# A cached attention decode step beside a squared-ReLU MLP: fewer key blocks scored on TensorE, products for 52 blocks on GpSimd

## The chip, the core and the metric

The kernel runs on one core of a Trainium2 chip. The metric is the time of one execution on the device, in microseconds; lower is better. The kernel before takes 193.13 us, the median of three runs (193.12 to 193.56).

## The reference

One token `x` of 512 values goes through two branches, which a scalar gate mixes.

```python
g = sigmoid((x * gate_w).sum(-1))
q = (x @ wq) as 32 heads of 128
scores = einsum("hd,hkd->hk", q, k_cache) * 128 ** -0.5     # 4096 keys a head
o = einsum("hk,hkd->hd", softmax(scores), v_cache)
a = o as 4096 values @ wo                                   # 4096 x 512
h = relu(x @ w1 + b1); b = (h * h) @ w2 + b2                # 512 -> 1376 -> 512
out = g * a + (1 - g) * b
```

All inputs are bf16. The K and V caches hold 32 MB each (4 MB for four heads), wq and wo 4 MB each, w1 and w2 1.4 MB each. Every byte is used once.

## The kernel before

**Quads.** The 32 heads are worked on four at a time: eight quads. The 128 partitions of a quad's K tile hold four heads of 32 partitions, and each partition holds 128 keys of 128 values, so a "block" is one key of each partition: 128 blocks a quad. V lies in the same way. K has three buffers (`Kt`), V two (`Vt`). The third K buffer first holds the MLP weights, the second V buffer wq, the first V buffer at the end wo, and the V tiles of the last two quads go into K buffers.

**Scores.** A score is the product of a key with the q of its head, summed over 128 values. It is made in two ways. For 48 blocks (`XB`) VectorE multiplies K by q, which is spread over the head's partitions in `qb` (`prods`, line 574, two times 24 blocks), and sums over the 128 values (`sums`, line 583). For the other 80 TensorE transposes a block (`transposes`, line 395), ScalarE moves eight transposed blocks at a time from PSUM to `kT` (`evac`, line 321), and TensorE multiplies each with the four q columns in `qc` (`scores`, line 405); VectorE copies that part of the scores out of PSUM (line 590) and takes the row maxima (line 597).

**Softmax and PV.** TensorE and VectorE bring the maxima of a head's 32 partitions together (`max_rows`, `gmax`, `max_cols`), ScalarE copies the negative maximum (line 325) and forms the exponentials and their sums (line 336), and TensorE multiplies V blocks by them (`pv`, line 437). At the end the denominators are summed (`den`, line 448), the result is normalised and regrouped (lines 636 to 641), and TensorE multiplies it with wo in five pieces (`attn_out`, line 506), each waiting for its own DMA. The last steps are `fin` (line 644), a transpose, a copy, and the DMA of 1 KB.

**q.** The q of all heads is first made as columns (128 matmuls, line 372), copied to `qc`, transposed, and spread over partitions by eight matmuls with the selector `selq`; ScalarE copies the result to `qb` (line 315).

**The MLP.** The 1376 hidden units are held as 8 columns of 128, one of 96 and 8 of 32 (`FG`, `FR`, `TX` by `QX`). The last, 256 rows of w2, are the extras: they are loaded as 32 rows of eight w2 rows (8 KB) into partitions 0 to 15 and 32 to 47 of `WX` by 8 DMAs with four rows each (line 252). `mlp_h` (lines 462 and 466) makes the units, VectorE's `mlp` squares them, `mlp_x` moves the extras to their partitions with the selector `selh`, and `mlp_out` (line 487) adds to the output. Its end (`s_ml`) releases the third K buffer.

**What sets the order.** Each engine follows a list written out by hand, with semaphores between engines. SP issues all large loads in this order: wq, K0, w1, w2 with its extras, K1, V0, K2 (waits for `s_ml`), K3, V1, K4, V2, K5, V3, K6, V4, K7, V5, V6, V7 in two halves, wo in five pieces. From K3 on, a K load waits until its buffer's quad has been transposed and multiplied (lines 221 and 222); a V load waits for the PV of two quads before (line 232). TensorE runs transposes and scores of quad i chunk by chunk, and between the chunks the max steps of quad i-1 and the PV of quads i-2 and i-3. VectorE works on quad i's products and sums with the maxima of quad i-1 in between. GpSimd only prepares constants in the first 9 us.

Of the kernel before, what the change touches and what calls it, by code (L numbers as in the profile page):

```python
# [5 lines left out]
def bass_gated_mix__gqa_block_cached__dense_activation_squared_relu__decode_kernel(  # L6
# [30 lines left out]
    FG = 8  # L37
    FR = 96
    F0 = FG * 128
    F1 = F0 + FR  # L40
    TX = 8
    QX = 32
    PX = 48
# [3 lines left out]
    XB = 48  # L47
    XH = XB // 2
# [8 lines left out]
    NR = 5  # L57
# [15 lines left out]
    with ctx:  # L73
# [18 lines left out]
        pr = sb("pr", [128, XH, 128], fp32)  # L92
        qb = sb("qb", [128, NQ, 128], bf16)
        qT = sb("qT", [NH, 128], bf16)
        selq = sb("selq", [NH, NQ, 128], bf16)
# [42 lines left out]
        pS = [pb(f"pS{i}", [128, 512], fp32) for i in range(2)]  # L138
# [8 lines left out]
        Q = pX[:, 0:NH]  # L147
# [4 lines left out]
        QR = [T[1], T[2]]  # L152
# [4 lines left out]
        def S(i):  # L157
            return pS[i % 2][:, 0:4 * YB].rearrange("p (b h) -> p b h", h=4)
# [24 lines left out]
        s_q = sem("s_q")  # L183
# [6 lines left out]
        s_qb = sem("s_qb")  # L190
        s_mu = sem("s_mu")
        s_sd = sem("s_sd")
# [22 lines left out]
        with nc.Block() as block:  # L215

            @block.sync
            def _(eng):
                def load_k(i):
                    if i >= NK:  # L220
                        eng.wait_ge(s_t, NC * (i - NK + 1))
                        eng.wait_ge(s_mu, 2 * (i - NK + 1))
# [4 lines left out]
                def load_v(i):  # L227
                    if i == 1:
                        eng.wait_ge(s_q, 1)
# [6 lines left out]
                    eng.wait_ge(s_mu, 2 * i)  # L236
# [32 lines left out]
            def _(eng):  # L269
# [4 lines left out]
                eng.memset(selq[:, :, :], 0.0).then_inc(s_id, 1)  # L274
                eng.memset(sel[:, :, :], 0.0).then_inc(s_id, 1)
                eng.memset(selm[:, :], -SCALE).then_inc(s_id, 1)
                eng.wait_ge(s_id, 6)
                for m in (ident, identf):
# [3 lines left out]
                eng.affine_select(out=selq[:, :, :], in_=selq[:, :, :], compare_op=ALU.not_equal, fill=1.0,  # L282
                                  base=0, pattern=[[-4, NQ], [-1, 4], [0, HP]], channel_multiplier=1)\
                   .then_inc(s_id, 1)
# [3 lines left out]
                eng.wait_ge(s_id, 10)  # L288
# [7 lines left out]
                for p, q in ((0, 0), (32, 16)):  # L296
                    eng.affine_select(out=selh[:, p:p + 16], in_=selh[:, p:p + 16], compare_op=ALU.not_equal,
                                      fill=1.0, base=-q, pattern=[[-1, 16]], channel_multiplier=1)\
                       .then_inc(s_hx, 1)

            @block.scalar
            def _(eng):
# [7 lines left out]
                eng.activation(xcol[:, :], xcolf[:, :], ACT.Copy).then_inc(s_xf, 1)  # L310
                eng.wait_ge(s_z, 1)
                eng.activation(ez[:, :], Z, ACT.Exp, scale=-1.0).then_inc(s_ez, 1)
                for g in range(2):
                    eng.wait_ge(s_qr, g + 1)
                    eng.activation(qb[:, 4 * g:4 * g + 4, :], QR[g][:, :].rearrange("p (j d) -> p j d", d=128), ACT.Copy).then_inc(s_qb, 1)  # L315

                def evac(n):
                    eng.wait_ge(s_t, n + 1)
                    if n >= NR:
                        eng.wait_ge(s_sc, n - NR + 1)  # L320
                    eng.activation(kT[:, n % NR, :], T[n % NT][:, :].bitcast(bf16), ACT.Copy).then_inc(s_ev, 1)  # L321

# [4 lines left out]
                def exps(j, hs_):  # L327
                    if hs_[0] == 0:
                        eng.wait_ge(s_nm, j + 1)
                        if j == 0:  # L330
                            eng.wait_ge(s_id, 13)
                        if j >= NE:
                            eng.wait_ge(s_pv, j - NE + 1)
                    for h in hs_:
# [5 lines left out]
                for i in range(NQ + 1):  # L340
                    for c in range(NC):
# [13 lines left out]
            def _(eng):  # L355
# [159 lines left out]
                for n in range((NQ + LAG) * NC):  # L515
                    i, c = n // NC, n % NC
                    if n < N:
                        transposes(n)
# [157 lines left out]
```

## Time and profile before

| | |
|---|---|
| median of the runs | 193.13 us |
| profiled execution | 193.35 us |
| its span | 192.1 us |
| HBM read | 78.32 MB, 408 GB/s over the span |
| TensorE, VectorE, ScalarE, GpSimd busy | 134.9, 134.7, 102.4, 7.9 us |
| mean granted TensorE clock | 0.663 |

A busy engine in this profile is one with an instruction in work; its waits are named by what released it. "DMA" in the slices and windows is the mean busy share of the core's 16 DMA engines. In the chain of work, the program is followed back from its last instruction, each time to what released it. DVE is VectorE, ACT ScalarE, PE TensorE and POOL GpSimd.

### The profile page before, as it was taken

How to read it: one execution, taken by the hardware profiler on the slowest of the kernel's cores; microseconds unless marked ns; L12 is line 12 of the kernel's file. 1: busy time of each engine (PE TensorE's matmuls, PEld its weight loads, DVE VectorE, ACT ScalarE, POOL GpSimd, SP SyncE). 2: the span in 40 equal slices, each digit the busy share in tenths (PEclk: the TensorE clock that was granted, in tenths of full speed). 3: DMA queues.
4: the chain of work that ended last, by engine and by line, in shares of the span. 5: the costliest groups of instructions: out<-in, count | busy, mean ns of one | idle time of the engine just before them, and what ended most of it. 6: DMA issues, size and time to landing. Idle time of an engine off the chain costs nothing.

```text
span 192.1 us, 6115 instructions
## 1 busy us (share of the span) xinstructions
PE 134.9 (70%) x2768; PEld 130.3 (68%) x2768; DVE 134.7 (70%) x157; ACT 102.4 (53%) x159; POOL 7.9 (4%) x21
## 2 busy tenths in 40 slices
PE   0128089997803996589979397939794988667954
PEld 0126089997703995579979397939794988667943
DVE  6410095999993999999999899939993899440010
ACT  2101050869961989637947766586648574904000
POOL 8800000000000000000000000000000000000000
PEclk9999999997885699555555555555555555555555
DMA  6999999999999999999999999999999999999981
GB/s 219 438 437 437 391 448 430 437 420 437 433 427 418 418 433 423 427 430 433 427 413 437 433 437 427 427 430 433 423 440 425 427 430 433 396 423 403 421 328 45
DMA packets 3823, 78.70 MB, mean 410 GB/s; under 512 B 467, under 2 KB 565, under 8 KB 822
## 3 DMA queue, kind: packets, MB, share of 16 engines
q1 hardware_dynamic: 3784, 78.32, 95.9%
q8 instruction: 21, 0.34, 0.7%
q14 instruction: 4, 0.03, 0.0%
q10 hardware_dynamic: 14, 0.01, 0.0%
HBM read 78.32 MB, written 0.00 MB: 408 GB/s over the span
## 4 chain that ended last, share of the span: by engine, by line
DMA 70%; PE 16%; DVE 11%; SPq 1%; issue 1%; DVEq 0%
DMA Kt<-in_A_k_cache_dram 40%; DMA Vt<-in_A_wo_dram 16%; DMA Kt<-in_B_w_dram 13%; PE T L395 7%; DVE pr L574 5%; DVE Sb L583 4%; PE pX L466 2%; PE pO L437 2%; PE pS L405 1%; DVE mp L597 1%; PE pX L487 1%; DVE Sb L590 1%; PE pX L462 1%; SPq L263 1%; PE pX L506 1%
## 5 line engine op out<-in xcount | busy, mean ns | idle before, releaser
L321 ACT ACTIVATE kT<-T 128x1024 bf16<-128x1024 bf16 x80 | 80.3, 1025 | 50.8 <-PE T L395 50.1
L395 PE MATMUL T<-ident,Kt 128*128 128x128 bf16 x640 | 74.3, 290 | 24.2 <-DMA Kt<-in_A_k_cache_dram 23.1
L395 PEld LDWEIGHTS T<-ident,Kt 128*128 128x128 bf16 x640 | 56.7, 131 | 25.1 <-DMA Kt<-in_A_k_cache_dram 23.6
L574 DVE TENSOR_TENSOR pr<-Kt,qb 128x3072 f32<-128x3072 bf16 x16 | 53.7, 3357 | 17.9 <-DMA Kt<-in_A_k_cache_dram 17.0
L583 DVE TENSOR_REDUCE Sb<-pr 128x12 f32<-128x1536 f32 x32 | 55.1, 1745 | 0.5
L405 PEld LDWEIGHTS pS<-qc,kT 128*128 128x128 bf16 x640 | 30.9, 111 | 4.4 <-ACT kT L321 4.4
L405 PE MATMUL pS<-qc,kT 128*128 128x4 bf16 x640 | 30.9, 170 | 3.5 <-ACT kT L321 3.2
L437 PE MATMUL pO<-E,Vt 128*128 128x4 bf16 x768 | 28.8, 166 | 3.8 <-DMA Vt<-in_A_v_cache_dram 3.8
L437 PEld LDWEIGHTS pO<-E,Vt 128*128 128x128 bf16 x768 | 25.5, 103 | 4.5 <-issue 4.0
L336 ACT ACTIVATE E<-Sb,nM 32x128 bf16<-32x128 f32 x32 | 18.4, 576 | 0.9
L590 DVE COPY Sb<-pS 32x80 f32<-32x80 f32 x32 | 7.5, 236 | 3.8 <-PE pS L405 3.0
L597 DVE TENSOR_REDUCE mp<-Sb 32x1 f32<-32x128 f32 x32 | 8.9, 277 | 1.6
L336 ACT ACTIVATION_READ_ACCUMULATOR E<-Sb,nM 32x1 f32 x32 | 8.0, 250 | 0.0
L437 PE MATMUL pO<-E,Kt 128*128 128x4 bf16 x256 | 7.3, 166 | 0.0
L437 PEld LDWEIGHTS pO<-E,Kt 128*128 128x128 bf16 x256 | 7.2, 105 | 0.0
L416 PE MATMUL pM<-identf,mp 128*4 128x128 f32 x8 | 2.9, 360 | 5.8 <-DVE mp L597 5.8
L315 ACT ACTIVATE qb<-T 128x512 bf16<-128x512 f32 x2 | 1.1, 594 | 9.1 <-PE T L381 9.1
L359 PE MATMUL pM<-ident,xrow 1*128 1x1 bf16 x4 | 0.3, 165 | 7.9 <-POOL sel L292 7.9
L359 PEld LDWEIGHTS pM<-ident,xrow 1*128 1x128 bf16 x4 | 0.2, 108 | 7.9 <-POOL sel L292 7.9
L506 PE MATMUL pX<-o,Vt 128*128 128x1 bf16 x128 | 3.9, 165 | 1.6 <-DMA Vt<-in_A_wo_dram 1.3
L506 PEld LDWEIGHTS pX<-o,Vt 128*128 128x128 bf16 x128 | 3.6, 104 | 1.9 <-DMA Vt<-in_A_wo_dram 1.5
L416 PEld LDWEIGHTS pM<-identf,mp 128*4 128x4 f32 x8 | 0.7, 82 | 6.1 <-DVE mp L597 6.1
(75 smaller groups left out, 61.6 us busy)
## 6 DMA issues: line engine op xcount, KB each, us to landing
Kt<-in_A_k_cache_dram SPq DMA_DIRECT2D x8, 4096.0 KB, 29.4
Vt<-in_A_v_cache_dram SPq DMA_DIRECT2D x6, 4096.0 KB, 21.7
Vt<-in_A_wq_dram SPq DMA_DIRECT2D x1, 4096.0 KB, 12.5
Kt<-in_A_v_cache_dram SPq DMA_DIRECT2D x1, 4096.0 KB, 32.2
Kt<-in_A_v_cache_dram SPq DMA_DIRECT2D x2, 2048.0 KB, 31.3
Vt<-in_A_wo_dram SPq DMA_DIRECT2D x3, 1024.0 KB, 27.6
Kt<-in_B_w_dram SPq DMA_DIRECT2D x1, 1376.0 KB, 25.8
Kt<-in_B_w_dram SPq DMA_DIRECT2D x1, 1024.0 KB
```

The source lines that it names most:

```text
L321: eng.activation(kT[:, n % NR, :], T[n % NT][:, :].bitcast(bf16), ACT.Copy).then_inc(s_ev, 1)
L336: eng.activation(E[a:b, j % NE, :, h], Sb[a:b, j % NS, :], ACT.Exp, bias=nM[a:b, j:j + 1], scale=SCALE, accum_out=RS[a:b, j:j + 1]).then_i ...
L395: mm = eng.transpose(T[n % NT][:, :].bitcast(bf16)[:, y * 128:(y + 1) * 128], Kt[:, i % NK, w * 128:(w + 1) * 128], ident[:, :])
L405: mm = eng.matmul(S(i)[:, c * TC + y, :], kT[:, n % NR, y * 128:(y + 1) * 128], qc[:, 4 * i:4 * i + 4], start=True, stop=True)
L416: eng.transpose(MT, mp[:, i, :], identf[:, :]).then_inc(s_mt, 1)
L437: mm = eng.matmul(pO[:, 4 * i:4 * i + 4], VT(i)[:, y * 128:(y + 1) * 128], E[:, i % NE, y, :], start=(y == 0), stop=(y == NB - 1))
L466: mm = eng.matmul(H[0:height(n), n:n + 1], units(w1_t[:, t, :], n), xcol[:, t:t + 1], start=False, stop=(t == 3), skip_group_check=True)
L506: mm = eng.matmul(acc[:, j:j + 1], wo_sb[:, t, j * 128:(j + 1) * 128], o2[:, t:t + 1], start=False, stop=(t == 31), skip_group_check=True)
L574: eng.tensor_tensor(pr[:, :, :], Kt[:, i % NK, u * XH * 128:(u + 1) * XH * 128] .rearrange("p (b d) -> p b d", b=XH), qb[:, i:i + 1, :].br ...
L583: eng.tensor_reduce(Sb[:, i % NS, u * XH + a:u * XH + b], pr[:, a:b, :], AX.X, ALU.add)\
L590: eng.tensor_copy(Sb[a:b, i % NS, XB:NB], S(i)[a:b, :, h]).then_inc(s_cp, 1)
L597: eng.tensor_reduce(mp[a:b, i, h:h + 1], Sb[a:b, i % NS, :], AX.X, ALU.max)\
```

## The change

Five things change together.

- The blocks of a quad are divided anew: GpSimd multiplies 52 blocks by q (four times 13, into two buffers `pg`), VectorE multiplies 28 (two times 14) and sums all 80, and TensorE transposes and scores 48 instead of 80 (six chunks instead of ten).
- VectorE's products read q from PSUM (`PQ`, a copy made once a quad), not from SBUF. The scores of TensorE's blocks have one PSUM bank instead of two and are copied out by ScalarE, not VectorE.
- q is made spread over the partitions from the start: ScalarE writes x into all 128 weight columns (`xb`), four matmuls of 512 columns a quad give q on every partition, ScalarE copies 32 partitions of each head to `qb`, and transposes of `qb` give the columns. The selector `selq` goes.
- The MLP's units become 9 columns of 128, one of 64 and 4 of 40; the w2 extras become 40 rows of four w2 rows (4 KB), loaded by 8 DMAs with five rows each.
- TensorE's order becomes plain: all transposes and scores of quad i, the max steps of quad i-1, PV of quad i-2. In quad 0 the MLP stands behind all transposes and scores. ScalarE and VectorE are ordered to suit.

```diff
-    FG = 8
-    FR = 96
+    FG = 9
+    FR = 64
-    TX = 8
-    QX = 32
-    PX = 48
+    TX = 4
+    QX = 40
+    PX = 52
-    XB = 48
-    XH = XB // 2
+    GP = 4
+    GB = 13
+    XP = 2
+    XH = 14
+    XB = GP * GB + XP * XH
...
-    NR = 5
+    NR = 4
...
+        pg = sb("pg", [128, 2, GB, 128], fp32)
+        xb = kT[:, 0, 0:512].rearrange("p (t n) -> p t n", t=4)
...
-        pS = [pb(f"pS{i}", [128, 512], fp32) for i in range(2)]
+        pS = pb("pS", [128, 512], fp32)
+        pQ = pb("pQ", [128, 512], fp32)
...
                     if i >= NK:
                         eng.wait_ge(s_t, NC * (i - NK + 1))
-                        eng.wait_ge(s_mu, 2 * (i - NK + 1))
+                        eng.wait_ge(s_mu, XP * (i - NK + 1))
+                        eng.wait_ge(s_pm, GP * (i - NK + 1))
...
-                    for p, q in ((0, 0), (32, 16)):
-                        eng.dma_start(WX[p + r:p + 16:4, :], w2_x[q + r:q + 16:4, :]).then_inc(s_w2, 16)
+                    for p, q in ((0, 0), (32, 20)):
+                        eng.dma_start(WX[p + r:p + 20:4, :], w2_x[q + r:q + 20:4, :]).then_inc(s_w2, 16)
...
+                for i in range(NQ):
+                    eng.wait_ge(s_k[i % NK], 16 * (i // NK + 1))
+                    eng.wait_ge(s_qb, 4 * (i + 1))
+                    for k in range(GP):
+                        n = GP * i + k
+                        if n >= 2:
+                            eng.wait_ge(s_ps, n - 1)
+                        eng.tensor_tensor(pg[:, n % 2, :, :], Kt[:, i % NK, k * GB * 128:(k + 1) * GB * 128]
+                                          .rearrange("p (b d) -> p b d", b=GB),
+                                          qb[:, i:i + 1, :].broadcast_to([128, GB, 128]), ALU.mult)\
+                           .then_inc(s_pm, 1)
...
+                eng.activation(xb, xcolf[:, :].rearrange("p (t o) -> p t o", o=1).broadcast_to([128, 4, 128]),
+                               ACT.Copy).then_inc(s_xf, 1)
...
-                for g in range(2):
-                    eng.wait_ge(s_qr, g + 1)
-                    eng.activation(qb[:, 4 * g:4 * g + 4, :], QR[g][:, :].rearrange("p (j d) -> p j d", d=128), ACT.Copy).then_inc(s_qb, 1)
+                for j in range(NQ):
+                    eng.wait_ge(s_qr, j + 1)
+                    for h in range(4):
+                        a, b = HP * h, HP * h + HP
+                        eng.activation(qb[a:b, j, :], T[j % NT][a:b, h * 128:(h + 1) * 128], ACT.Copy)\
+                           .then_inc(s_qb, 1)
...
+                def score_copy(i):
+                    eng.wait_ge(s_sc, NC * (i + 1))
+                    for h in range(4):
+                        a, b = HP * h, HP * h + HP
+                        eng.activation(Sb[a:b, i % NS, XB:NB], S[a:b, :, h], ACT.Copy).then_inc(s_cp, 1)
...
                 for i in range(NQ + 1):
+                    if i < NQ:
+                        for c in range(NC):
                             evac(i * NC + c)
+                        score_copy(i)
...
+                    if i >= 1:
+                        neg_max(i - 1)
+                        exps(i - 1)
...
+                for j in range(NQ):
+                    if j >= NT:
+                        eng.wait_ge(s_qb, 4 * (j - NT + 1))
+                    for t in range(4):
+                        mm = eng.matmul(T[j % NT][:, :], xb[:, t, :], wq_sb[:, t, j * 512:(j + 1) * 512],
+                                        start=(t == 0), stop=(t == 3))
                     mm.then_inc(s_qr, 1)
+                    if j >= 1:
+                        q_columns(j - 1)
+                q_columns(NQ - 1)
...
+                for i in range(NQ + 2):
+                    if i < NQ:
+                        for c in range(NC):
+                            transposes(i * NC + c)
+                            if c >= 2:
+                                scores(i * NC + c - 2)
+                        scores(i * NC + NC - 2)
+                        scores(i * NC + NC - 1)
+                    if i == 0:
+                        mlp_h()
+                        mlp_x()
+                        mlp_out()
                     if 1 <= i < NQ + 1:
+                        max_rows(i - 1)
+                        max_cols(i - 1)
+                    if i == NQ + 1:
+                        den()
+                    if i >= 2:
+                        pv(i - 2, 0, NB // 2)
+                        pv(i - 2, NB // 2, NB)
...
+                def q_psum(i):
+                    eng.wait_ge(s_qb, 4 * (i + 1))
+                    eng.tensor_copy(PQ[:, i % 4, :], qb[:, i, :]).then_inc(s_pq, 1)
...
-                                      qb[:, i:i + 1, :].broadcast_to([128, XH, 128]), ALU.mult).then_inc(s_mu, 1)
+                                      PQ[:, i % 4:i % 4 + 1, :].broadcast_to([128, XH, 128]), ALU.mult)\
+                       .then_inc(s_mu, 1)
...
+                def psums(i, k):
+                    n = GP * i + k
+                    eng.wait_ge(s_pm, n + 1)
...
+                    eng.tensor_reduce(Sb[:, i % NS, k * GB:(k + 1) * GB], pg[:, n % 2, :, :], AX.X, ALU.add)\
+                       .then_inc(s_ps, 1)
...
                     if i < NQ:
                         prods(i, 0)
                     if i >= 1:
+                        psums(i - 1, 3)
                         smax(i - 1)
                     if i < NQ:
-                        sums(i, 0, 0)
+                        sums(i, 0)
+                        psums(i, 0)
                     if i >= 1:
                         gmax(i - 1)
                     if i < NQ:
-                        sums(i, 0, 1)
-                    if i == 0:
-                        mlp()
-                    if i < NQ:
                         prods(i, 1)
-                        sums(i, 1, 0)
-                        sums(i, 1, 1)
+                        psums(i, 1)
+                        sums(i, 1)
+                        if i + 1 < NQ:
+                            q_psum(i + 1)
+                        if i == 0:
+                            mlp()
+                        psums(i, 2)
```

More of the change, by code (lines that the diff above doesn't have):

```diff
@@ L325, in neg_max, with exps @@
                     eng.activation(nM[:, j:j + 1], MB[:, j:j + 1], ACT.Copy).then_inc(s_nm, 1)
[L327 to L334, printed above, removed]
+                def exps(j):
+                    eng.wait_ge(s_nm, j + 1)
+                    if j == 0:
+                        eng.wait_ge(s_id, 11)
+                    if j >= NE:
+                        eng.wait_ge(s_pv, j - NE + 1)
+                    for h in range(4):
                         a, b = HP * h, HP * h + HP
@@ L586, in smax @@
                 def smax(i):
-                    eng.wait_ge(s_sc, NC * (i + 1))
-                    for h in range(4):
-                        a, b = HP * h, HP * h + HP
-                        eng.tensor_copy(Sb[a:b, i % NS, XB:NB], S(i)[a:b, :, h]).then_inc(s_cp, 1)
                     if i == 0:
-                        eng.wait_ge(s_id, 11)
-                    eng.wait_ge(s_sd, 4 * (i + 1))
+                        eng.wait_ge(s_id, 9)
+                    eng.wait_ge(s_sd, XP * (i + 1))
```

142 lines of the change are left out of this document (49 added, 93 removed).

## The prediction

> **What bounds the kernel now.** I read the page first: its totals, its slices, its DMA queues and its chain of work.
>
> ```profile
> span 192.1 us, 6115 instructions
> ...
> PE 134.9 (70%) x2768; PEld 130.3 (68%) x2768; DVE 134.7 (70%) x157; ACT 102.4 (53%) x159; POOL 7.9 (4%) x21
> ...
> DMA  6999999999999999999999999999999999999981
> ...
> q1 hardware_dynamic: 3784, 78.32, 95.9%
> q8 instruction: 21, 0.34, 0.7%
> ...
> DMA 70%; PE 16%; DVE 11%; SPq 1%; issue 1%; DVEq 0%
> ```
>
> No engine is above 70%, but the 16 DMA engines are full from the second slice to the last but one, and the chain is 70% DMA. The change keeps all 78.32 MB. So it can win only where the DMA engines aren't all busy, which is the last slices, and it loses if an engine becomes slower than the DMA stream. I cut the end into microseconds (after the clock column: DMA share, GB/s) and read the timeline there.
>
> ```profile
> 184.00:185.00 1.00, 0.41 (x9) 0.31 (x10) 0.19 (x1) 0.00 (x0) 0.00 (x0) 0.50 0.76 317
> 185.00:186.00 1.00, 1.00 (x43) 1.00 (x41) 0.00 (x0) 0.00 (x0) 0.00 (x0) 0.50 0.73 305
> 186.00:187.00 1.00, 0.71 (x27) 0.62 (x24) 0.00 (x0) 0.00 (x0) 0.00 (x0) 0.50 0.68 274
> 187.00:188.00 1.00, 0.83 (x31) 0.84 (x32) 0.00 (x0) 0.00 (x0) 0.00 (x0) 0.50 0.47 178
> 188.00:189.00 1.00, 0.18 (x7) 0.10 (x4) 0.00 (x0) 0.00 (x0) 0.00 (x0) 0.50 0.24 92
> ```
>
> ```profile
> 172.55 0.17 ACT L325 ACTIVATE nM<-pM 128x1 f32<-128x1 f32 x1 [4.44 <-PE pM L422]
> ...
> 175.25 1.85 PE L448 MATMUL pM<-RS,hone 128*128 128x8 f32 x8 [1.26 <-issue]
> ...
> 182.32 0.25 DVE L636 SCALAR_TENSOR_TENSOR onorm<-pO,gcol,rden 128x32 bf16<-128x32 f32 x1 [4.82 <-PE pO L437]
> 184.84 1.86 PE L506 MATMUL pX<-o,Vt 128*128 128x1 bf16 x64 [0.28 <-DVE o L641]
> 189.04 1.01 PE L506 MATMUL pX<-o,Vt 128*128 128x1 bf16 x32 [0.86 <-DMA Vt<-in_A_wo_dram]
> ```
>
> The engines run dry one after another: 0.24+0.27+0.32+0.53+0.76 = 2.1 us of mean idle time, while the last matmuls wait until 189.04 for wo from the latest engines. TensorE was ready at 184.84. What ends the program is how much later than the mean the fullest DMA engine is.
>
> **Part 1, the w2 extras.** Before, 8 DMAs carry four rows of 8 KB each; after, 8 DMAs carry five rows of 4 KB.
>
> ```profile
> Kt<-in_B_w_dram SPq DMA_DIRECT2D x8, 32.0 KB
> ...
> 0.00:60.51 60.51, 31.95 (x605) 30.56 (x605) 36.21 (x52) 24.97 (x36) 7.90 (x21) 0.93 0.98 412
> ```
>
> By the number of rows four engines get 64 KB each; one engine moves 78.32 MB / (0.959 x 192.1 us x 16) = 26.6 GB/s, so that is 2.46 us. The second row bears it out. By 60.51 us, when K quad 2 has landed, 24.9 MB had moved, where the queue up to that quad (five transfers of 4096 KB, 2752 KB of MLP weights) holds 23.8 MB: the mean engine is 1.1 MB / 16 = 70 KB ahead of the latest. After: five engines with 32 KB, 1.23 us; the 96 KB that go into the even transfers cost every engine 0.23 us. The four gain 1.0 us, the eleven others lose 0.23, the fifth loses 1.46. [...]
>
> **Part 2, TensorE's instructions.** Transposes and scores fall from 640 to 384 each, q from 137 matmuls to 40, the MLP from 154 to 127: 2768 becomes 2132, each with a weight load. TensorE has nine tenths of all instructions, so I assign the 21 instruction packets to it: 23% fewer is 16, five less. One takes 0.007 x 192.1 x 16 / 21 = 1.0 us of one engine. Spread evenly that is 0.3 us; where late engines have one less, 1.0.
>
> Sum at the DMA end: if the latest engines are the four of the extras, -1.0; if they are those with most instruction packets, -1.0+0.23 = -0.8; if the fifth is one of the latest, +1.46-1.0 = +0.5; with all unevenness gone, -2.1. I take -0.9, between the two likely readings, since 0.24 of 16 engines in the last microsecond is four engines.
>
> **Part 3, VectorE.** It loses 20 blocks of products and the score copies, and gains sums over 32 blocks and one copy of q.
>
> ```profile
> L583 DVE TENSOR_REDUCE Sb<-pr 128x12 f32<-128x1536 f32 x32 | 55.1, 1745 | 0.5
> L574 DVE TENSOR_TENSOR pr<-Kt,qb 128x3072 f32<-128x3072 bf16 x16 | 53.7, 3357 | 17.9 <-DMA Kt<-in_A_k_cache_dram 17.0
> L597 DVE TENSOR_REDUCE mp<-Sb 32x1 f32<-32x128 f32 x32 | 8.9, 277 | 1.6
> L590 DVE COPY Sb<-pS 32x80 f32<-32x80 f32 x32 | 7.5, 236 | 3.8 <-PE pS L405 3.0
> L602 DVE TENSOR_REDUCE gm<-pM 4x1 f32<-4x128 f32 x8 | 2.2, 279 | 0.7 <-PE pM L416 0.5
> ...
> 60.53 3.36 DVE pr L574
> ...
> 76.91 3.36 DVE pr L574
> ...
> 112.92 0.35 PE pO L437 x13
> ...
> 149.27 3.36 DVE L574 TENSOR_TENSOR pr<-Kt,qb 128x3072 f32<-128x3072 bf16 x1 [3.43 <-DMA Kt<-in_A_k_cache_dram]
> ```
>
> From 1536 and 128 elements (1745 and 277 ns) a sum costs 1.043 ns an element and 144 ns. Per quad now: 2x3.36+4x1.75+4x0.24+4x0.28+0.28 = 16.0, and one quad took 76.91-60.53 = 16.4. After: products 2x1792 elements, 2x2.02 = 4.05; sums of 14 blocks 2x2.01 = 4.03; of 13 blocks 4x1.88 = 7.5; maxima 1.4; copy of q 0.25 (like L590); 17.2, with the same 0.4 of gaps r = 17.6 us. That the product reads q from PSUM I cost at nothing: L602 reads PSUM and takes 279 ns where L597 takes 277.
>
> This is hidden only while K comes slower. Quad 2 landed at 60.5, quad 7 at 149.25, 17.75 us a quad: VectorE at 17.6 follows just so, with quad 7 starting at about 149.3. From there its r less 0.4, then sums 1.9, maxima 1.1, max over rows and columns to the ScalarE copy 1.7, copy and exps at most 3.5 (PV of quad 6, 128 x 27 ns, beside them), denominators 1.9, PV of quad 7 3.5: 13.6. PV ends at 180.1 where it now ends at 182.3. If VectorE alone sets the pace, PV ends at 60.5+6r-0.4+13.6 = 73.7+6r; 2.5 us of regrouping, 3.7 of output matmuls and 2.0 of finish make the span 81.9+6r. That overtakes the DMA end (191.2) at r = 18.2: a cover of 0.6 us a quad, and each 0.1 beyond costs 0.6.
>
> **Part 4, GpSimd.** It makes four products of 13 blocks (1664 elements) a quad; no row shows one.
>
> ```profile
> L291 POOL MEMSET E<- 128x2048 bf16 x1 | 1.8, 1794 | 0.0
> L282 POOL TENSOR_SCALAR_AFFINE_SELECT selq<-selq 32x1024 bf16<-32x1024 bf16 x1 | 1.3, 1280 | 0.0
> ```
>
> A write alone is 0.88 ns an element, 1.46 us a product. One input is 1.25; two inputs one after another are 2.5, so 4.2 us; with a write of its own after them 3.4, 5.6 us. I take 4.2, by the row that reads an input. VectorE uses a product at least 6 us after it frees the buffer, so only the sum counts: 4x4.2 = 16.6 below 17.6. From 4.55 us on GpSimd sets r above 18.2. [...]
>
> **Part 5, ScalarE, the head and the queues.**
>
> ```profile
> L321 ACT ACTIVATE kT<-T 128x1024 bf16<-128x1024 bf16 x80 | 80.3, 1025 | 50.8 <-PE T L395 50.1
> L336 ACT ACTIVATE E<-Sb,nM 32x128 bf16<-32x128 f32 x32 | 18.4, 576 | 0.9
> L315 ACT ACTIVATE qb<-T 128x512 bf16<-128x512 f32 x2 | 1.1, 594 | 9.1 <-PE T L381 9.1
> L325 ACT ACTIVATE nM<-pM 128x1 f32<-128x1 f32 x8 | 1.3, 166 | 4.4 <-PE pM L422 4.4
> ...
> 13.41 3.56 PE L372 MATMUL pX<-xcol,Vt 128*128 128x1 bf16 x128 [0.42 <-DMA Vt<-in_A_wq_dram]
> 24.17 3.36 DVE L574 TENSOR_TENSOR pr<-Kt,qb 128x3072 f32<-128x3072 bf16 x1 [6.38 <-DMA Kt<-in_A_k_cache_dram]
> ...
> 28.81 4.39 PE pX L466 x68
> ...
> 34.36 0.88 PE T L395 x8
> ...
> 38.83 1.81 PE pX L487 x68
> ...
> 40.65 1.53 SPq L225 DMA_DIRECT2D Kt<-in_A_k_cache_dram  x2
> 83.31 0.33 SPq L233 DMA_DIRECT2D Vt<-in_A_v_cache_dram  x1
> ```
>
> ScalarE drops four evacuations a quad (4.1 us) and gains four score copies (about 1): idle already, worth nothing. New q: 32 copies of 128 elements at (594-166)/511 x 127 + 166 = 0.27 us are 8.7 us after wq's arrival at 13.4 and a first group, so q is complete at 24.0 at the earliest, against K quad 0 at 24.17. If TensorE takes its 2048 columns a group at the pace of the transposes (8x128 columns in 0.88 us), a group is 1.76 us and q complete at 13.4+8x1.76+1.1 = 28.6. I take 25, nearer the copies, as a wide matmul loads its weights once for 512 columns. VectorE and GpSimd start with quad 0's q alone. The MLP now stands behind 48 blocks of transposes and scores (25+7.4+1 = 33.4) and, on VectorE, behind seven operations: mlp_h with 70 matmuls to 37.9, VectorE's part and the selection to 40, mlp_out with 56 to 41.5. So K quad 2 is issued at about 41.5 (now 40.65), at 45 by the late end; wq to V of quad 0 are 19.6 MB, which keep the engines busy to about 47. The late end would also hold VectorE at the MLP, so that quad 2 starts at 62.6 instead of 60.5 and r may be 17.9 at most. SP's next waits: K of quad 3 needs GpSimd's fourth product, about 42; V of quad 2 needs PV of quad 0, now in quad 2's own pass behind products, sums and maxima (9.3), one max matmul (0.6) and 3.5 of its own, 60.5+13.4 = 74 instead of 83.31; wo likewise earlier. Each queued transfer is issued before the engines run dry; cost nothing.
>
> Sum: span 192.1-0.9 = 191.2. The profiled execution took 193.35, 1.25 outside the span and 0.2 above the median of 193.13: 192.2.
>
> **The rivals.** (a) The latest DMA engine isn't relieved (the fifth is one of the latest, or it takes no part): 193.1 (192.8 to 193.6). For: no view names engines. Against: the 70 KB. (b) GpSimd becomes the bound, from 4.55 us a product on, because VectorE's sums then wait for it. At 5.0 r is 20, the span 201.9, the time about 203; at 5.6, 217. For: the bound 5.6; against: 4.2. (c) VectorE is lengthened while GpSimd works, or by PSUM reads. From 3% on it decides; at 5% r is 18.5 and the time 194; at 10%, 19.3 and 199. For: GpSimd was idle here, so no row excludes it, and a late q would take half of the cover. [...] (d) The drain becomes even: -2.1, 191.0.
>
> **How the numbers follow.** Forecast 0.51 (191.7 to 192.6), (a) 0.20, (b) 0.13, (c) 0.11, (d) 0.05. The first and (d) are the faster ones, less a little that falls within 0.3% (0.58 us, about what a measurement of this kernel can tell from no change): 0.54; same 0.21; slower 0.25. The range leaves out (b) and the upper part of (c), and below the best of (d): 191.2 to 195.0.
>
> **What would show it.** Right: GpSimd's products under 4.4 us; VectorE's quads 17.6 apart or less where K is there; about 16 instruction packets; V of quad 2 issued near 74; the last wo matmuls still released by DMA, near 188.1. Wrong: VectorE idle before its sums of GpSimd's products, quads over 18.2 us, or output matmuls that follow the PV end without waiting for wo.

## The result, and the profile after

The changed kernel takes 191.94 us (191.71 to 192.43, five runs) beside 193.30 us (193.12 to 194.15) for the kernel before in the same five rounds: a ratio of 0.9925, with a 95% interval of 0.9898 to 0.9951. A second set of five runs gave 191.98 beside 193.26, 0.9936 (0.9918 to 0.9954). The forecast was 192.2. The profiled execution took 192.43 us, with a span of 191.1; it is the longest of its five, whose median span is 190.6. The profiled one of before took 193.35 with 192.1.

First the page: its totals, its slices of DMA and its DMA queues.

```profile
span 191.1 us, 4828 instructions
PE 105.6 (55%) x2132; PEld 92.1 (48%) x2132; DVE 139.5 (73%) x147; ACT 82.9 (43%) x191; POOL 112.1 (59%) x51
...
DMA  6999999999999999999999999999999999999991
...
q1 hardware_dynamic: 3768, 78.32, 96.3%
q8 instruction: 16, 0.26, 0.6%
```

GpSimd went from 7.9 to 112.1 us of work, and the DMA engines are still full from the second slice to the last but one. So the time is decided at the end once more. There are 16 instruction packets, not 21. The groups of instructions, with busy time and mean ns of one, give the new operations their prices.

```profile
L312 POOL TENSOR_TENSOR pg<-Kt,qb 128x1664 f32<-128x1664 bf16 x32 | 106.9, 3344 | 52.3 <-DVE Sb L614 21.9
L614 DVE TENSOR_REDUCE Sb<-pg 128x13 f32<-128x1664 f32 x32 | 59.8, 1871 | 0.0
L597 DVE TENSOR_TENSOR pr<-Kt,pQ 128x1792 f32<-128x1792 bf16 x16 | 32.1, 2006 | 15.8 <-DMA Kt<-in_A_k_cache_dram 15.8
L607 DVE TENSOR_REDUCE Sb<-pr 128x14 f32<-128x1792 f32 x16 | 32.1, 2009 | 0.3
```

GpSimd's product takes 3.34 us, and VectorE never waits before the sum that uses it (0.0). The only long wait of VectorE in these groups, 15.8 us, is for K. The timeline of VectorE shows where: each quad's first product, and behind it in brackets the idle time.

```profile
77.24 2.00 DVE L597 TENSOR_TENSOR pr<-Kt,pQ 128x1792 f32<-128x1792 bf16 x1
...
93.92 2.00 DVE L597 TENSOR_TENSOR pr<-Kt,pQ 128x1792 f32<-128x1792 bf16 x1
...
129.48 2.02 DVE L597 TENSOR_TENSOR pr<-Kt,pQ 128x1792 f32<-128x1792 bf16 x1 [2.13 <-DMA Kt<-in_A_k_cache_dram]
...
148.92 2.02 DVE L597 TENSOR_TENSOR pr<-Kt,pQ 128x1792 f32<-128x1792 bf16 x1 [2.66 <-DMA Kt<-in_A_k_cache_dram]
```

Where K is there a quad takes 93.92-77.24 = 16.68 us, and quads 6 and 7 wait for K again: the pace is that of the DMA engines. SP's timeline has K of quad 2 and V of quad 2:

```profile
38.97 0.80 SPq L233 DMA_DIRECT2D Kt<-in_A_k_cache_dram  x2
...
73.85 0.33 SPq L241 DMA_DIRECT2D Vt<-in_A_v_cache_dram  x1
```

The end, cut into microseconds (after the clock: DMA share, GB/s), and TensorE's timeline there:

```profile
184.00:185.00 1.00, 1.00 (x42) 1.00 (x42) 0.00 (x0) 0.00 (x0) 0.00 (x0) 0.50 0.83 340
185.00:186.00 1.00, 1.00 (x43) 1.00 (x41) 0.00 (x0) 0.00 (x0) 0.00 (x0) 0.50 0.76 313
186.00:187.00 1.00, 0.60 (x23) 0.51 (x20) 0.00 (x0) 0.00 (x0) 0.00 (x0) 0.50 0.62 236
187.00:188.00 1.00, 0.54 (x20) 0.55 (x21) 0.00 (x0) 0.00 (x0) 0.00 (x0) 0.50 0.16 61
188.00:189.00 1.00, 0.50 (x18) 0.44 (x15) 0.00 (x0) 0.00 (x0) 0.00 (x0) 0.50 0.00 0
```

```profile
175.78 0.39 PE L474 MATMUL pM<-RS,hone 128*128 128x8 f32 x2 [1.01 <-issue]
...
182.08 0.22 PE L463 MATMUL pO<-E,Kt 128*128 128x4 bf16 x2 [2.11 <-issue]
...
187.46 0.80 PE L532 MATMUL pX<-o,Vt 128*128 128x1 bf16 x24 [0.86 <-DMA Vt<-in_A_wo_dram]
188.75 0.35 PE L532 MATMUL pX<-o,Vt 128*128 128x1 bf16 x8 [0.50 <-issue]
```

The last microsecond of before, with 0.24 of the DMA engines still busy, is gone. The last matmuls still wait for wo, but until 187.46 instead of 189.04. Not all of these 1.6 us arrive: the last eight matmuls wait another 0.50 us for nothing that the profile names, so the last matmul ends at 189.1 instead of 190.05. Near the end TensorE has two more such waits, of 1.01 us in the denominators and 2.11 us two matmuls before the end of PV. They come back below.

### The profile page after: what moved, and what is told of

It is laid out like the page before. It is cut to its first block, busy times and chain, and to the rows that moved or that the text cites. A ratio compares the mean times of both kernels' runs of the same rounds, so it can differ in the third digit from the quotient of the medians.

```text
span 191.1 us, 4828 instructions
## 1 busy us (share of the span) xinstructions
PE 105.6 (55%) x2132; PEld 92.1 (48%) x2132; DVE 139.5 (73%) x147; ACT 82.9 (43%) x191; POOL 112.1 (59%) x51
## 5 line engine op out<-in xcount | busy, mean ns | idle before, releaser
L312 POOL TENSOR_TENSOR pg<-Kt,qb 128x1664 f32<-128x1664 bf16 x32 | 106.9, 3344 | 52.3 <-DVE Sb L614 21.9
L343 ACT ACTIVATE kT<-T 128x1024 bf16<-128x1024 bf16 x48 | 45.2, 1033 | 38.1 <-PE T L418 38.1
L614 DVE TENSOR_REDUCE Sb<-pg 128x13 f32<-128x1664 f32 x32 | 59.8, 1871 | 0.0
L418 PE MATMUL T<-ident,Kt 128*128 128x128 bf16 x384 | 38.4, 274 | 26.7 <-DMA Kt<-in_A_k_cache_dram 24.9
L418 PEld LDWEIGHTS T<-ident,Kt 128*128 128x128 bf16 x384 | 32.1, 126 | 27.4 <-DMA Kt<-in_A_k_cache_dram 25.3
L597 DVE TENSOR_TENSOR pr<-Kt,pQ 128x1792 f32<-128x1792 bf16 x16 | 32.1, 2006 | 15.8 <-DMA Kt<-in_A_k_cache_dram 15.8
L607 DVE TENSOR_REDUCE Sb<-pr 128x14 f32<-128x1792 f32 x16 | 32.1, 2009 | 0.3
L431 PE MATMUL pS<-qc,kT 128*128 128x4 bf16 x384 | 17.4, 167 | 8.9 <-ACT kT L343 8.3
L431 PEld LDWEIGHTS pS<-qc,kT 128*128 128x128 bf16 x384 | 15.0, 101 | 11.6 <-ACT kT L343 11.4
L403 PE MATMUL T<-Vt,kT 128*128 128x512 bf16 x32 | 9.5, 437 | 0.2 <-DMA Vt<-in_A_wq_dram 0.2
```

The lines of the kernel that those rows point to most:

```text
L312: eng.tensor_tensor(pg[:, n % 2, :, :], Kt[:, i % NK, k * GB * 128:(k + 1) * GB * 128] .rearrange("p (b d) -> p b d", b=GB), qb[:, i:i + 1 ...
L403: mm = eng.matmul(T[j % NT][:, :], xb[:, t, :], wq_sb[:, t, j * 512:(j + 1) * 512], start=(t == 0), stop=(t == 3))
L418: mm = eng.transpose(T[n % NT][:, :].bitcast(bf16)[:, y * 128:(y + 1) * 128], Kt[:, i % NK, w * 128:(w + 1) * 128], ident[:, :])
L431: mm = eng.matmul(S[:, c * TC + y, :], kT[:, n % NR, y * 128:(y + 1) * 128], qc[:, 4 * i:4 * i + 4], start=True, stop=True)
L597: eng.tensor_tensor(pr[:, :, :], Kt[:, i % NK, a * 128:(a + XH) * 128] .rearrange("p (b d) -> p b d", b=XH), PQ[:, i % 4:i % 4 + 1, :].bro ...
L607: eng.tensor_reduce(Sb[:, i % NS, a:a + XH], pr[:, :, :], AX.X, ALU.add).then_inc(s_sd, 1)
```

## The experiments

At the outset two theories of the gain stood against each other. X: the latest DMA engines are those of the w2 extras, and five rows of 4 KB instead of four of 8 KB relieved them. P: the latest are the engines that also carry TensorE's instruction packets, of which there are five fewer. A third question is the cover: how much slower GpSimd and VectorE may be before it shows. The runs came in three sets, each beside its own runs of the kernel before (193.19, 193.26 and 193.08). "Landing" below is the end of the transfer of wo's fourth piece in the chain of waits or the timeline, 188.99 before and 187.41 after.

**The old extras in the changed kernel.**

```diff
-    FG = 9
+    FG = 8
-    FR = 64
+    FR = 96
-    TX = 4
+    TX = 8
-    QX = 40
+    QX = 32
-    PX = 52
+    PX = 48
...
-                    for p, q in ((0, 0), (32, 20)):
-                        eng.dma_start(WX[p + r:p + 20:4, :], w2_x[q + r:q + 20:4, :]).then_inc(s_w2, 16)
+                    for p, q in ((0, 0), (32, 16)):
+                        eng.dma_start(WX[p + r:p + 16:4, :], w2_x[q + r:q + 16:4, :]).then_inc(s_w2, 16)
...
```

> The kernel after, with the MLP's units and the w2 extras laid out as before: 32 rows of 8 KB by 8 DMAs of four rows (64 KB on each of four engines) instead of 40 rows of 4 KB by 8 DMAs of five. Theory X (the last DMA engines are those of the extras): the four end 1.23 us later, 0.23 less for the even part, so about 1.0 us more than the kernel after, 192.9. Theory P (the last engines are those that also fetch TensorE's instructions, and the extras lie on other engines): the even part is 6 KB an engine smaller, so 0.2 us less or equal, 191.7 to 191.9, as long as the four don't become the last.

Measured 192.72, ratio 0.9977 (0.9969 to 0.9986), landing 188.35; the chain of waits, and the windows of the end:

```profile
148.13 40.22 DMA Vt<-in_A_wo_dram
```

```profile
187.00:188.00 1.00, 0.03 (x2) 0.00 (x0) 0.00 (x0) 0.00 (x0) 0.00 (x0) 0.50 0.25 80
188.00:189.00 1.00, 0.60 (x22) 0.60 (x23) 0.00 (x0) 0.00 (x0) 0.00 (x0) 0.50 0.03 12
```

That is 0.74 us above the second set of the changed kernel, so with 17 packets the extras' engines are late, as X has it; 0.25 of 16 engines, where the changed kernel has 0.16, fits four of them. But 0.5 us of the gain is left without the new extras, which X can't give.

**No extras.** The hidden units beside the first 1280 become one column of 96, and w2 comes in even transfers alone.

```diff
-    FG = 9
+    FG = 10
-    FR = 64
+    FR = 96
-    TX = 4
+    TX = 0
...
-                for r in range(4):
-                    for p, q in ((0, 0), (32, 20)):
-                        eng.dma_start(WX[p + r:p + 20:4, :], w2_x[q + r:q + 20:4, :]).then_inc(s_w2, 16)
...
```

> The kernel after with no w2 extras: ten unit columns of 128 and one of 96, the 160 rows that were extras now in even transfers (10 KB more on every engine, 32 KB less on five). Without the zeroing of the extras' tile, their selector and their 8 DMAs. Theory X: the five engines end 32 KB - 10 KB = 22 KB earlier, 0.8 us less, 191.1. Theory P: the engines that fetch instructions carry 10 KB more, 0.38 us more, 192.3.

Measured 192.56, ratio 0.9964 (0.9952 to 0.9976). X's 191.1 is excluded. It is near P's 192.3, but not for P's reason alone: the median span is 190.9, against 190.7 for the changed kernel, and the rest of the difference lies outside the span, 1.67 us against 1.3. No view shows why. So even transfers end no earlier than five rows of extras.

**More instructions.** 624 additional score matmuls repeat a chunk's first block, whose score they write again; this is extra work.

```diff
-                    for y in range(TC):
+                    for y in [0] * 13 + list(range(TC)):
```

> The kernel after, with 13 scores of each chunk of eight done twice over (13 matmuls of four columns more a chunk, 624 in all, same results), so that TensorE has 2756 matmuls, nearly as many as before (2768), about 21 instruction packets instead of 16, and some 2 us more work a quad, which TensorE has free. Theory X: five packets more are spread over 16 engines, 0.3 us more, 192.2. Theory P: the engines that fetch get up to one packet more each, 1.0 to 1.6 us more, 193.0 to 193.5.

Measured 193.40, ratio 1.0011 (1.0003 to 1.0020), landing 189.06. The page's DMA queues:

```profile
q8 instruction: 21, 0.34, 0.7%
```

and the windows of its end:

```profile
187.00:188.00 1.00, 0.88 (x32) 0.89 (x32) 0.00 (x0) 0.00 (x0) 0.00 (x0) 0.50 0.42 160
188.00:189.00 1.00, 0.13 (x5) 0.04 (x2) 0.00 (x0) 0.00 (x0) 0.00 (x0) 0.50 0.25 96
```

Five more packets, made by TensorE's matmuls alone, take back the whole gain. TensorE's busy time rises to 120.3 us, still below the 134.9 of before, and the last matmuls still wait for wo. A packet takes 0.007 x 192.1 x 16 / 21 = 1.0 us of one engine; spread over 16 engines five would cost 0.3 us. They cost 1.4, so a few engines carry them. The windows bear this out: 0.42 and 0.25 are nearly the 0.47 and 0.24 of the kernel before, although the extras now lie on five engines with half the load: while the 40 packets of 4 KB run in the trace of the changed kernel, five are under way at a time beside eleven of 32 KB, and in that of the kernel before the last packets of 8 KB run four at a time beside twelve of 32 KB. So the 0.24, which the prediction read as the extras' four engines, comes back with the packets alone.

**Eight rows of 8 KB.** Four rows ran on four engines before and five on five after, so eight rows are taken to lie on eight engines, with 64 KB each: an estimate, since no view names an engine.

```diff
-    FG = 9
+    FG = 6
-    FR = 64
+    FR = 96
-    TX = 4
+    TX = 8
-    QX = 40
+    QX = 64
-    PX = 52
+    PX = 64
...
-                    for p, q in ((0, 0), (32, 20)):
-                        eng.dma_start(WX[p + r:p + 20:4, :], w2_x[q + r:q + 20:4, :]).then_inc(s_w2, 16)
+                    for p, q in ((0, 0), (32, 32)):
+                        eng.dma_start(WX[p + r:p + 32:4, :], w2_x[q + r:q + 32:4, :]).then_inc(s_w2, 16)
...
```

> The kernel after with more extras, on eight engines: 64 rows of 8 KB by 8 DMAs of eight rows (64 KB on each of eight engines), six unit columns of 128 and one of 96; 352 KB, 22 KB an engine, leave the even transfers. Theory X: the engines of the extras carry 32 - 22 = 10 KB more than in the kernel after, 0.4 us more, 192.3. Theory P, if the eight engines are those that fetch nothing: the fetching engines end 22 KB = 0.83 us earlier, 191.1, faster than both kernels; if some of the eight do fetch, slower than the kernel after by up to 1.6.

Measured 193.29, ratio 1.0011 (0.9998 to 1.0023), landing 188.71. The windows of the end:

```profile
187.00:188.00 1.00, 1.00 (x44) 1.00 (x41) 0.00 (x0) 0.00 (x0) 0.00 (x0) 0.50 0.17 70
188.00:189.00 1.00, 0.50 (x19) 0.42 (x17) 0.00 (x0) 0.00 (x0) 0.00 (x0) 0.50 0.09 33
189.00:190.00 1.00, 0.77 (x29) 0.68 (x26) 0.16 (x1) 0.00 (x0) 0.00 (x0) 0.50 0.08 16
```

A share of 0.09 and 0.08 is one or two engines of 16, not eight. This suggests that one or two of the engines added carried more than the others already, and are late now.

**The changed kernel once more**, as the second set's own standard.

> The kernel after, unchanged, run beside the next ones for a firmer base: 0.9925 of the time before, about 191.8; no theory has another number.

Measured 191.98, ratio 0.9936, landing 187.77, 17 packets. So the number of packets in the profile varies by one, and the landing by 0.4.

**The new extras in the kernel before.**

```diff
-    FG = 8
+    FG = 9
-    FR = 96
+    FR = 64
-    TX = 8
+    TX = 4
-    QX = 32
+    QX = 40
-    PX = 48
+    PX = 52
...
-                    for p, q in ((0, 0), (32, 16)):
-                        eng.dma_start(WX[p + r:p + 16:4, :], w2_x[q + r:q + 16:4, :]).then_inc(s_w2, 16)
+                    for p, q in ((0, 0), (32, 20)):
+                        eng.dma_start(WX[p + r:p + 20:4, :], w2_x[q + r:q + 20:4, :]).then_inc(s_w2, 16)
...
```

> The kernel before with one part of the change alone: the MLP's units and w2 extras as after (40 rows of 4 KB by 8 DMAs of five rows). TensorE keeps 80 blocks, so 20 or 21 instruction packets. Theory X (the extras' engines are the last ones): four engines end 1.0 us earlier, 192.2. Theory P (the last ones are those that fetch TensorE's instructions): 6 KB more on each, 0.2 us more, 193.4. The runs so far (moving the extras back costs 1.0, but so does having none, 0.8, and five more packets cost 1.6) fit a mixture: with 21 packets the fetching engines end last, and with 16 the extras' four would. By that, 193.2 to 193.4 here.

Measured 193.32, ratio 1.0003 (0.9992 to 1.0014), with 21 packets, landing 188.64. By themselves the new extras bring nothing. With the first experiment: the change without the new extras -0.5, the new extras alone 0, both -1.3. With 21 packets the new extras give 193.40 in the changed kernel and 193.32 in the one before, so what else changed is worth nothing measurable, and the -0.5 is put down to the packets. This fits two groups of engines that were nearly equally late before, where taking load from one leaves the other.

**Six rows, and heavier rows on five engines.** These two ask on how many engines the extras may lie. The first has six rows of 6 KB in each DMA, the second five rows of 6 KB.

```diff
-    FG = 9
+    FG = 8
-    TX = 4
+    TX = 6
-    QX = 40
+    QX = 48
-    PX = 52
+    PX = 56
...
-                        eng.dma_start(WX[p + r:p + 20:4, :], w2_x[q + r:q + 20:4, :]).then_inc(s_w2, 16)
+                        eng.dma_start(WX[p + r:p + 24:4, :], w2_x[q + r:q + 24:4, :]).then_inc(s_w2, 16)
...
```

> The kernel after with 48 rows of 6 KB by 8 DMAs of six rows (48 KB on each of six engines), eight unit columns of 128 and one of 64; 8 KB an engine leave the even transfers. Of eight engines some fetch TensorE's instructions, as the run with eight rows showed by ending 1.5 us later. If the sixth engine is none of them: 0.3 us less than the kernel after, 191.7. If it is: that engine carries two packets and 48 KB, 1.8 - 0.3 = 1.5 us more, 193.3.

Measured 193.13, ratio 1.0006 (0.9995 to 1.0017), landing 188.57: the whole gain is gone with a sixth row. The windows of its end:

```profile
187.00:188.00 1.00, 0.78 (x30) 0.69 (x26) 0.00 (x0) 0.00 (x0) 0.00 (x0) 0.50 0.07 29
188.00:189.00 1.00, 0.39 (x14) 0.39 (x15) 0.00 (x0) 0.00 (x0) 0.00 (x0) 0.50 0.04 16
```

A share of 0.07, and of 0.04 up to 188.57, is about one engine of 16.

```diff
-    FG = 9
+    FG = 8
-    FR = 64
+    FR = 112
-    TX = 4
+    TX = 6
```

> The kernel after with a little more on the same five engines: 40 rows of 6 KB by 8 DMAs of five rows (48 KB each instead of 32), eight unit columns of 128 and one of 112; 5 KB an engine leave the even transfers. By the mixed theory (five engines with extras, others with two instruction packets each, both now ending close together) the fetching engines gain 0.19 us and the five lose 0.4: 191.8 to 192.2, no difference that can be measured. Theory X: 0.4 us more, 192.4.

Measured 192.38, ratio 0.9963 (0.9951 to 0.9976), landing 187.16. Its median span, 190.8, is that of the changed kernel; most of the 0.4 us lies outside the span again (1.60 against 1.3). So, with one engine counted for each row, five engines bear 48 KB each without a later end (landing 187.41 with 32 KB), and 48 KB on a sixth cost 1.0 us of span (191.8). That the sixth is one that also fetches instructions is what the runs suggest; no view names an engine. That five and six rows differ so much would fit a sixth engine that is the same in all eight DMAs; this was not shown.

**q from SBUF.** VectorE's products read `qb` instead of its copy in PSUM.

```diff
-                                      PQ[:, i % 4:i % 4 + 1, :].broadcast_to([128, XH, 128]), ALU.mult)
+                                      qb[:, i:i + 1, :].broadcast_to([128, XH, 128]), ALU.mult)
```

> The kernel after, with VectorE's products reading q from SBUF instead of PSUM (the copy to PSUM stays), so that they have two SBUF inputs while GpSimd's products read SBUF. Theory without contention: quads 16.7 us apart as after, 191.9. Theory with a port that one engine holds for a whole instruction: each of VectorE's two products a quad waits for a GpSimd product of 3.3 us, or that one for 2.0; quads 16.7 + 2 x 1.7 = 20 apart or more, and by my sum (81.9 + 6r, less 0.5) a span of 201 or more, 202 to 206.

Measured 192.17, ratio 0.9943 (0.9923 to 0.9963). The groups, and VectorE's timeline:

```profile
L312 POOL TENSOR_TENSOR pg<-Kt,qb 128x1664 f32<-128x1664 bf16 x32 | 135.4, 4255 | 25.2 <-DMA Kt<-in_A_k_cache_dram 18.8
...
L597 DVE TENSOR_TENSOR pr<-Kt,qb 128x1792 f32<-128x1792 bf16 x16 | 36.5, 2279 | 9.5 <-DMA Kt<-in_A_k_cache_dram 9.5
```

```profile
77.33 2.76 DVE L597 TENSOR_TENSOR pr<-Kt,qb 128x1792 f32<-128x1792 bf16 x1
...
94.77 2.77 DVE L597 TENSOR_TENSOR pr<-Kt,qb 128x1792 f32<-128x1792 bf16 x1
...
166.60 1.89 DVE L614 TENSOR_REDUCE Sb<-pg 128x13 f32<-128x1664 f32 x1 [1.02 <-POOL pg L312]
```

The two engines do get in each other's way: GpSimd's product goes from 3.34 to 4.26 us, VectorE's from 2.01 to 2.28 in the mean. But quads are 94.77-77.33 = 17.44 us apart, not the 20 that I had expected, and quad 7 still waits 1.83 us for K. So only what quad 7 itself is delayed counts: VectorE waits 1.02 us there for GpSimd's last product. PV ends at 183.6, and the last matmuls follow without a wait for wo. The 0.2 us of time that this costs are within the intervals.

**GpSimd slowed by a quarter.** Three of each product's 13 blocks are made twice, with a wait between; this is extra work.

```diff
+                        eng.tensor_tensor(pg[:, n % 2, 0:3, :], Kt[:, i % NK, k * GB * 128:(k * GB + 3) * 128]
+                                          .rearrange("p (b d) -> p b d", b=3),
+                                          qb[:, i:i + 1, :].broadcast_to([128, 3, 128]), ALU.mult)\
+                           .then_inc(s_pw, 1)
+                        eng.wait_ge(s_pw, n + 1)
...
```

> The kernel after, with GpSimd making three of the 13 blocks of each product twice (and waiting for itself in between): about 3.34 + 0.8 to 1.0 = 4.2 to 4.4 us a product instead of 3.34, which is what I had taken. By my sum four of them (16.9 to 17.5) stand beside VectorE's quad, and the quad may take 18.2 before the DMA stream is overtaken: no change, 191.9 within 0.3. If GpSimd already sets the end: more by 6 x 4 x 0.9 = 20 us.

Measured 192.30, ratio 0.9951 (0.9935 to 0.9968). The groups of GpSimd:

```profile
L318 POOL TENSOR_TENSOR pg<-Kt,qb 128x1664 f32<-128x1664 bf16 x32 | 106.9, 3340 | 2.5
...
L313 POOL TENSOR_TENSOR pg<-Kt,qb 128x384 f32<-128x384 bf16 x32 | 29.2, 912 | 22.9 <-DMA Kt<-in_A_k_cache_dram 19.5 <-DVE Sb L620 3.4
```

A pair of 0.91+3.34 us and a short wait is a product of about 4.3 us, and the time is the same within the intervals. The last product holds VectorE for 1.10 us and PV ends at 183.8, so that here too the last matmuls follow without a wait for wo. So the cover at the end is used up at a product of about 4.3 us; the forecast had 4.55.

**GpSimd slowed by half.** The same with seven of 13 blocks; the lines are set against the run before.

```diff
-                        eng.tensor_tensor(pg[:, n % 2, 0:3, :], Kt[:, i % NK, k * GB * 128:(k * GB + 3) * 128]
+                        eng.tensor_tensor(pg[:, n % 2, 0:7, :], Kt[:, i % NK, k * GB * 128:(k * GB + 7) * 128]
```

> The kernel after, with GpSimd making seven of the 13 blocks of each product twice. With three blocks a pair took 4.28 us (0.91 + 3.34) and cost nothing; by those two sizes 896 elements take 1.88, a pair 5.2 us, four of them 20.9 a quad, beyond the 18.2 at which my sum lets the quads overtake the DMA stream. By the sum (81.9 + 6r, less 0.5 for the earlier start of quad 2) the span is 206.8 and the time 208. If the K loads (about 19.4 us a quad) set the pace and only the excess of GpSimd over them counts: 6 x 1.5 = 9 us more, 201. If GpSimd is hidden anyway: 192.

Measured 212.80 in two runs, ratio 1.1020 (1.1001 to 1.1039). In the waits of VectorE (us in total, times, longest), and in its timeline:

```profile
DVE Sb L620 <- POOL pg L318: 32.0, 23, 3.4
```

```profile
61.55 2.01 DVE L603 TENSOR_TENSOR pr<-Kt,pQ 128x1792 f32<-128x1792 bf16 x1
...
82.58 2.01 DVE L603 TENSOR_TENSOR pr<-Kt,pQ 128x1792 f32<-128x1792 bf16 x1
```

VectorE waits for GpSimd, and a quad takes 21.03 us: rival (b)'s mechanism, at its place. My expectation of 208 was 4.8 us low. It had quad 2 start at 60.0, where it starts at 61.55, since GpSimd is behind from quad 0 on; the quads were taken 20.9 apart and not 21.03, 0.7 us over five; and from the start of quad 7, at 166.74, to the end of the span it takes 2.5 us more than the sum, for VectorE waits another 3.4 us there for the last product, which the sum did not have.

**What TensorE's unnamed waits are.** The runs with other numbers of matmuls answer this too. In the changed kernel the waits named "issue" stand 2 matmuls before the end of the denominators, 2 before the end of PV, and 8 before the end of wo: 2+126 = 128 and 2+1+4+120 = 127 matmuls apart. With five rows of 6 KB the MLP has nine matmuls more, and the same waits stand nine earlier:

```profile
181.62 0.46 PE L463 MATMUL pO<-E,Kt 128*128 128x4 bf16 x11 [1.03 <-issue]
...
187.93 0.59 PE L532 MATMUL pX<-o,Vt 128*128 128x1 bf16 x17 [0.16 <-issue]
```

Without extras there are 28 fewer, and they stand 102 before the end of PV and 107 before that of wo: 128 apart, and 28 places later, counted in steps of 128 (2+128-28 = 102). Its timeline:

```profile
176.76 1.16 PE L443 MATMUL pO<-E,Kt 128*128 128x4 bf16 x38 [0.67 <-issue]
178.36 1.87 PE L443 MATMUL pO<-E,Kt 128*128 128x4 bf16 x64 [0.45 <-DMA Kt<-in_A_v_cache_dram]
...
183.03 1.31 PE L505 MATMUL pX<-o,Vt 128*128 128x1 bf16 x43 [0.51 <-issue]
```

So they hang on the count of instructions: 128 matmuls with their weight loads are one packet of 0.26 MB / 16 = 16 KB, and the page's 2132 matmuls in 16 packets give nearly the same, 133 to a packet. Not every unnamed wait is of this kind: the 1.26 us before the denominators of the kernel before stand at the same place with the new extras there, 27 matmuls fewer.

Nor does each such place have a wait. In the changed kernel four of about 16 do, the fourth with 1.78 us at 76.05. With the old extras there are 27 matmuls more, so that the first two of the three places lie 21 matmuls before the end of PV in quad 6 and 29 before it in quad 7. Both are passed without a wait, though the DMA engines are full:

```profile
169.91 3.57 PE L463 MATMUL pO<-E,Kt 128*128 128x4 bf16 x128
...
178.56 1.87 PE L463 MATMUL pO<-E,Kt 128*128 128x4 bf16 x64 [1.66 <-DMA Kt<-in_A_v_cache_dram]
```

With GpSimd slowed by half the DMA engines have almost nothing to do at the end, and TensorE passes the same places without a wait; its timeline, and the windows there:

```profile
200.82 3.55 PE L469 MATMUL pO<-E,Kt 128*128 128x4 bf16 x128
...
205.95 3.58 PE L538 MATMUL pX<-o,Vt 128*128 128x1 bf16 x128 [0.29 <-DVE o L678]
```

```profile
200.00:202.00 2.00, 2.00 (x50) 2.00 (x51) 0.36 (x1) 0.00 (x0) 0.00 (x0) 0.50 0.03 8
202.00:204.00 2.00, 2.00 (x82) 2.00 (x79) 0.00 (x0) 0.00 (x0) 0.00 (x0) 0.50 0.00 0
```

8 GB/s for 2 us is 16 KB, one packet, alone. Earlier in the same run, at 79.62 with the DMA engines full, TensorE waits 2.40 us at the place that has 1.78 us in the changed kernel. So it can wait for its next packet while the DMA engines are full, and did not at the end of this run, where they are free. That the packet stands in line behind data on its engine is the likely reason; no view shows that line, nor why most places are passed without a wait.

## Why the prediction was right, point by point

- **The bound.** Right: DMA engines full as before, and the time decided by the last pieces of wo.
- **Part 1, the extras, and the reading "the latest engines are the four of the extras, -1.0".** Wrong alone: 0 in the kernel before (193.32). It is worth 0.7 us only once the packets are fewer (192.72 to 191.98). The 70 KB were read rightly for their moment and wrongly for the end: VectorE's first product of quad 2, which waits for K, starts at 60.53 in the kernel before and at 59.80 there with the new extras, and in the changed kernel at 60.12 and at 61.24 with the old ones, which fits extras' engines that are the latest at that time. That these are four before and five after is in the traces (four packets of 8 KB, five of 4 KB at a time); that the five include the four, as "the fifth loses 1.46" takes it, no run shows. At the end the late engines are there without the old extras too (0.25 after 188.00 with 624 more matmuls). The even part's +0.23 was not measured by itself: without any extras, where 10 KB more on every engine would be 0.38 by the same price, the span is 0.2 longer.
- **Part 2, packets.** Right in their number (16) and their owner: 624 matmuls make five. Their price by the page after is 0.006 x 191.1 x 16 / 16 = 1.1 us, beside 1.0 before, both from a share of one digit; in the traces the packets take 0.95 to 1.11 us before and 1.02 to 1.12 after. "Where late engines have one less, 1.0": without the new extras -0.5 (192.72 beside 193.19), and together with the extras the last pieces of wo land 1.2 to 1.6 us earlier.
- **The sum of the DMA end, -0.9, "between the two likely readings".** The term that was mis-sized. It is not one reading or the other: by the experiments both groups were late, both were relieved, and the time fell by 1.3 (193.26 to 191.98). That is 0.3 below the forecast of 192.2 and inside the range. That the number is so near is in part luck: the -0.9 stood between two readings of which neither, taken alone, gives it.
- **Part 3, VectorE.** The parts were right (2.01 for 2.02, 1.87 for 1.88, q in PSUM at nothing). Their sum, 2x2.01+2x2.01+4x1.87+1.4+0.25 = 17.2, came out as 16.68, since neighbouring instructions overlap (the product of 2.00 us at 77.24 is followed at 79.17), where I had added 0.4 of gaps. So the cover against K was larger than forecast, and quads 6 and 7 wait for K.
- **Part 4, GpSimd.** 3.34 us, below the 4.2 taken and inside the bounds. The limit of 4.55 was a little high: at 4.3 the last product is the first to show (1.10 us in quad 7), since it has no later quad to hide behind, and at 5.2 GpSimd set the pace, as rival (b) had it.
- **Part 5, the head and the end.** q was complete at 24.9 (taken as 25; its 32 matmuls of 512 columns have 32 weight loads, as taken), V of quad 2 was issued at 73.85 (forecast 74), and K of quad 2 at 38.97, before the forecast 41.5. PV ended at 182.3, not 180.1: the waits of 1.01 and 2.11 us for instructions were in no step. Without them it would be about 180.0, and not 3.1 us earlier, since the second half of the last V lands only at 178.1, a step that the prediction's path did not have either; with the old extras, where neither wait occurs, that half is the last thing PV waits for and PV ends at 180.4. That this is nearly the forecast 180.1 is luck. The waits for instructions left 0.86 us of cover between the engines' end and that of the DMA, and a delay of 1 us in quad 7 uses it up. "Each queued transfer is issued before the engines run dry" held: the slices stay at 9.
- **The rivals.** (a) is excluded by the time; what it described appears with the sixth row (193.13). (c), the lengthening of VectorE, is absent with q in PSUM (2.01 us, forecast 2.02) and present with q in SBUF, where it is 14% of VectorE's products (2.28 us) and 27% of GpSimd's (4.26) but, since quad 7 waits for K, 0.2 us of time. (d), an even drain worth 2.1, did not come even without extras.

## What to carry to other kernels

In this kernel, whose DMA engines are full, instructions were DMA traffic too: 128 matmuls were a packet of 16 KB on the same engines as the data, and 624 matmuls more took the time from 191.98 to 193.40 us. So fewer matmuls can shorten the last transfers even where TensorE is far from being the bound. Look at the end engine by engine, as far as the shares allow: two groups that are equally late hide each other, so that one edit alone brings nothing or little (0, and -0.5) and both together bring 1.3 us. And a cover worked out from engine work alone should leave room for waits such as those of 0.2 to 3.0 us here, where an instruction packet ends.

## What the runs showed of the hardware

TensorE's unnamed waits near the end stand 127 or 128 matmuls apart and move with the number of matmuls. In these runs they take 0.2 to 3.0 us, come at some of these places only, and were not seen at the end of the one run whose DMA engines are free there. GpSimd's product of two bf16 inputs into fp32 took 912, 1887 and 3340 ns for 384, 896 and 1664 elements, about 1.9 ns an element and 0.18 us. With q in PSUM VectorE's product took 2.01 us in the mean and GpSimd's 3.34; with q in SBUF they took 2.28 and 4.26. What stays open is the time outside the span: 1.67 and 1.60 us with no extras and with five rows of 6 KB, about 1.3 in the others. No view shows why.
